# Channel attention into a gated feed-forward: the second chunk of v transposed on TensorE, and the last row group finished in two column halves

## The chip, the core and the metric

The kernel runs on one core of a Trainium2 chip. The metric is the device time of one execution in microseconds. A time is the median of several executions; the profile is of one execution.

## What is computed

Two stages follow each other. The first is channel attention over B = 4 batches of N = 6016 rows and C = 256 channels; the second is a feed-forward layer with a sigmoid gate over all 24064 rows, with 1536 hidden columns.

```
qn = q / (norm(q, axis=rows) + 1e-6)
kn = k / (norm(k, axis=rows) + 1e-6)
s  = kn.T @ qn / tau                       # 256 x 256 per batch, tau = 1
a  = softmax(s, last axis)
x  = v @ a                                 # 6016 x 256 per batch, rows of all batches joined
out = (sigmoid(x @ w_gate) * (x @ w_val)) @ w_out
```

Inputs and output are float32 in DRAM. The kernel computes its products in bfloat16 with float32 sums.

## The kernel before, in words

**Staging.** The product `v @ a` is never made by itself: for each batch the 256x256 matrix a is multiplied into the two weight matrices (`gh`: G = a w_gate and H = a w_val, in three column groups of 512, twelve pieces in all). What remains per batch is `sigmoid(v G) * (v H)` and the product with w_out. A batch has 47 row tiles of 128 rows, taken in NCH = 12 chunks: eleven of four tiles (512 rows) and a last one of three tiles (384 rows).

**A chunk.** `glu` (L404) does one of FC = 12 steps of a chunk, one for each 128 hidden columns: two products into a gate buffer and two into a val buffer of PSUM, each 512 columns wide, a sigmoid on ScalarE (L423) and a multiplication on VectorE (L424) that writes the hidden values hT. There are two gate buffers (pool psg) and two val buffers (psv), so a step can begin only when the step two before it has been read out of them. The moving operand of these products is v transposed, vT. `out_mms` (L430) does the product with w_out for the chunk before: per row tile twelve products of 256 columns, added up in one PSUM buffer (L440); `flush` (L446) copies the finished tile to SBUF on VectorE (L450) and, after the last tile of a chunk, stores the whole chunk from the SP queue (L452).

**Where vT comes from.** `load_v` (L103) loads a chunk of v through the GpSimd queue and casts it to bfloat16 on the way. `transpose_v` (L384) makes vT of it. It has two ways: a DMA transpose issued on SP (L391), or, when it is given a PSUM tile, eight TensorE products with the identity (L394) whose result is copied out in halves, one by VectorE (L398), one by ScalarE (L399; in the only call of this kind, for chunk 0 of batch 0, that copy is issued at L505).

**The order of work.** The schedule is written out by hand; every engine carries out its list in the order of the program. The start (L461 to L514) takes in q and k of batch 0, forms the scores and the softmax and the first five pieces of `gh`; the other seven follow the first seven glu steps of chunk 0 (L576, L577). In the loads' list on GpSimd come all q and k of batch 0, v of chunk 0, then the weights (L137 to L145): gate and val of column groups 0 and 1, v of chunk 1, gate and val of group 2, and w_out. `side_work` (L517) lists what is done beside the glu steps, by slot (chunk x 12 + step): the loads of v two chunks ahead, the transpose of v one chunk ahead (L529: at step 2 of each chunk, and for the first chunk of batch 0 at step 0), and all of the next batch's scores and norms. SP's list holds just the transposes and the stores, in turn.

**The end.** After the last chunk's glu steps nothing is left but its own out product: L585 to L587 go through its three row tiles, twelve products each, copy each tile, and store the three tiles together (384 KB).

Of the kernel before, what the change touches and what calls it, by code (L numbers as in the profile page):

```python
# [9 lines left out]
FP32 = mybir.dt.float32  # L10
BF16 = mybir.dt.bfloat16
# [6 lines left out]
def kernel(  # L18
# [20 lines left out]
    nc = tc.nc  # L39
    P = nc.NUM_PARTITIONS  # L40
# [4 lines left out]
    B, N, C = q.shape  # L45
# [3 lines left out]
    CB = C // P  # L49
    FC = DFF // P  # L50
    FG = 512
    NFG = DFF // FG
    TPC = 4
    CH = TPC * P
    NCH = (NT + TPC - 1) // TPC
    groups = [(t, min(TPC, NT - t)) for t in range(0, NT, TPC)]
# [4 lines left out]
    def rows(x, b):  # L61
        return x[b].rearrange("(p t) c -> p t c", p=P)

    out_rows = out.rearrange("(b p t) c -> b p t c", b=B, p=P)

    def pool(name, bufs, **kw):
        return ctx.enter_context(tc.tile_pool(name=name, bufs=bufs, **kw))
# [10 lines left out]
    opool = pool("opool", 2)  # L78
    psg = pool("psg", 2, space=PSUM)
    psv = pool("psv", 2, space=PSUM)  # L80
    pso = pool("pso", 2, space=PSUM)
    pss = pool("pss", 1, space=PSUM)
    psm = pool("psm", 1, space=PSUM)
# [19 lines left out]
    def load_v(b, ci):  # L103
        t0, nt = groups[ci]
        v_sb = vpool.tile([P, TPC, C], BF16, tag="v", name="v_sb")
        nc.gpsimd.dma_start(out=v_sb[:, :nt, :], in_=rows(v, b)[:, t0 : t0 + nt, :])  # L106
        vs[b, ci] = v_sb


    t0, nt = groups0[0]  # L110
# [24 lines left out]
    w_sb = [[consts.tile([P, CB, FG], BF16, name=f"w_{n}{fg}") for fg in range(NFG)] for n in ("gate", "val")]  # L135
    w_out_sb = consts.tile([P, FC, C], BF16)
    for fg in range(NFG):  # L137
        if fg == NFG - 1:
            load_v(0, 1)
        for w, src in enumerate((moe_w_gate, moe_w_val)):  # L140
            nc.gpsimd.dma_start(  # L141
                out=w_sb[w][fg],
                in_=src.rearrange("(t p) f -> p t f", p=P)[:, :, ds(fg * FG, FG)],
            )
    nc.gpsimd.dma_start(out=w_out_sb, in_=moe_w_out.rearrange("(t p) c -> p t c", p=P))  # L145


# [254 lines left out]
    hts = {}  # L402
# [25 lines left out]
    ffn = {}  # L428

    def out_mms(b, ci, n0, n1):  # L430

        t0, nt = groups[ci]
        hT = hts[b, ci]
        for n in range(n0, min(n1, nt * FC)):
            s, f = divmod(n, FC)
            if n == 0:
                ffn[b, ci] = opool.tile([P, TPC, C], FP32, tag="osb", name="out_sb")
            if f == 0:
                ffn["ps"] = pso.tile([P, C], FP32, tag="o", name="ps_o")
            mm(ffn["ps"], hT[:, f, ds(s * P, P)], w_out_sb[:, f, :], f == 0, f == FC - 1)  # L440
            if f == FC - 1:
                pending.append((ffn[b, ci], s, ffn["ps"], b, ci))
# [3 lines left out]
    def flush():  # L446
        while pending:
            out_sb, s, ps, b, ci = pending.pop(0)
            t0, nt = groups[ci]
            nc.vector.tensor_copy(out=out_sb[:, s, :], in_=ps)  # L450
            if s == nt - 1:
                nc.sync.dma_start(out=out_rows[b][:, t0 : t0 + nt, :], in_=out_sb[:, :nt, :])  # L452


    def busy(n):

        ps = psg.tile([P, CH], FP32, tag="g", name="ps_busy")
        for _ in range(n):
            mm(ps, ones_bf, ones_wide, True, True)
# [57 lines left out]
    def side_work(b):  # L517


        side = {}  # L520

        def at(slot, fn, *a):
            side.setdefault(divmod(slot, FC), []).append((fn, a))

        for ci in range(NCH):
            nb, nci = (b, ci + 1) if ci + 1 < NCH else (b + 1, 0)
            lb, lci = (b, ci + 2) if ci + 2 < NCH else (b + 1, ci + 2 - NCH)
            if nb < B:
                at(ci * FC + (0 if (b, ci) == (0, 0) else 2), transpose_v, nb, nci)  # L529
            if lb < B:  # L530
                at(ci * FC + 0, load_v, lb, lci)
        n = b + 1
        if n == B:
            return side
        first, last = (14 if b == 0 else 0), 8 * FC
        for g, (t0, nt) in enumerate(groups):
            s0 = first + g * (last - first) // NCH
            at(max(0, s0 - 20), load_qk, n, t0, nt)
            for u in range(nt):
                at(first + (t0 + u) * (last - first) // NT, score, n, t0, u)  # L540
            if g == 0:
                at(s0, acc_start, n)
            for i, (fn, w) in enumerate(((acc_square, 0), (acc_add, 0), (acc_square, 1), (acc_add, 1))):
                at(s0 + 1 + 2 * i, fn, n, g, w)
        for i in range(6):
            at(8 * FC + 2 + i, acc_fold, n, *divmod(i, 3))
        at(9 * FC + 9, norms_mm, n)
        for ci, s, *call in (
            (9, 0, wide_sqrt, n),
            (9, 2, wide_inv, n, 0),  # L550
            (9, 3, wide_inv, n, 1),
            (10, 0, wide_scale, n),
            (10, 0, exps, n, 0),
            (10, 0, exps, n, 1),
        ):
            side.setdefault((ci, FC + s), []).append((call[0], call[1:]))
        at(11 * FC + 0, sums_both, n)
        at(11 * FC + 0, gh_tiles, n)
        for i in range(len(gh_order)):
            at(11 * FC + min(i + 1, FC - 1), gh, n, i, *((pss, "s"), (psm, "m"))[i % 2])  # L560
        return side


    prev = None
    for b in range(B):
        side = side_work(b)
        for ci in range(NCH):
            block = b + 1 < B and ci in (9, 10)
            for f in range(FC):
                glu(b, ci, f)  # L570
                flush()
                if prev is not None and not block:
                    out_mms(*prev, f * TPC, (f + 1) * TPC)
                for fn, a in side.get((ci, f), ()):
                    fn(*a)
                if (b, ci) == (0, 0) and f < len(gh_order) - 5:  # L576
                    gh(0, 5 + f, pso, "o")  # L577
            if prev is not None and block:
                for s in range(TPC):
                    for fn, a in side.get((ci, FC + s), ()):  # L580
                        fn(*a)
                    out_mms(*prev, s * FC, (s + 1) * FC)
                    flush()
            prev = (b, ci)
    for s in range(groups[NCH - 1][1]):  # L585
        out_mms(*prev, s * FC, (s + 1) * FC)
        flush()  # L587


# [33 lines left out]
```

## Time and profile before

| what | us |
|---|---|
| median of 3 executions | 833.98 |
| the three executions | 835.4, 832.1, 833.98 |
| the profiled execution, its own time | 835.4 |
| span of the profiled execution, first to last instruction | 833.3 |
| busy: TensorE products | 816.1 |
| busy: VectorE | 588.5 |
| busy: ScalarE | 391.2 |
| DMA transposes on SP: 47; issue to landing, min / median / max | 3.3 / 3.7 / 16.8 |
| stores of out on SP: 48; issue to landing, min / median / max | 2.3 / 2.9 / 7.9 |

All times inside the profile are counted from the start of the span. The names in it are PE for TensorE's products, PEld for its weight loads, DVE for VectorE, ACT for ScalarE, POOL for GpSimd, SPq for SP's queue of DMA issues. A row such as `PE L88 MATMUL ps_gate<-vT,gh_G` means: a product at line 88 (the helper that issues every product) that writes ps_gate and reads vT and gh_G. Products overlap one another, so the time from one start to the next is shorter than the duration of one. In the DMA rows q0 is the queue of the loads that GpSimd issues, q1 that of SP.

### The profile page before, as it was taken

The page shows a single profiled execution, that of the slowest core. Times are in us where ns is not written, and L with a number is a line of the kernel's source. Part 1 is how long each engine was busy: PE and PEld are TensorE (multiplying, and loading weights), DVE is VectorE, ACT ScalarE, POOL GpSimd, SP SyncE. Part 2 cuts the span into 40 slices and gives each one's busy share as a digit, 9 for nine tenths or more (in the row PEclk, how much of TensorE's full clock was granted, in tenths as well). Part 3 has the DMA queues.
Part 4 walks back from the last instruction along what each step waited for, and adds up shares of the span by engine and source line. Part 5 has one row for each costly group of instructions (what it writes and reads, how often), then busy time and mean ns, then how long its engine had stood idle before and what let it go on. Part 6 is the DMA issues. An engine that isn't in the chain of part 4 may idle for free.

```text
span 833.3 us, 13748 instructions
## 1 busy us (share of the span) xinstructions
PE 816.1 (98%) x5184; PEld 502.0 (60%) x5198; DVE 588.5 (71%) x1021; ACT 391.2 (47%) x643; POOL 83.4 (10%) x159
## 2 busy tenths in 40 slices
PE   7889899999999999999999999999999999999998
PEld 4546566666665666665566666666566566666666
DVE  6567777787667777778767777777766666666664
ACT  4654344446644444444654444444655444444442
POOL 5522100002101100000221010000000000000000
PEclk9999999999999999999999999999999999999999
DMA  9999832335947423322975353223322423322111
GB/s 210 206 179 202 139 64 51 80 70 103 178 84 133 95 52 89 61 52 57 181 140 104 85 116 64 51 48 89 64 51 65 79 52 85 67 49 73 42 35 71
DMA packets 79794, 77.43 MB, mean 93 GB/s; under 512 B 51824, under 2 KB 56688, under 8 KB 79728
## 3 DMA queue, kind: packets, MB, share of 16 engines
q0 software_dynamic: 23920, 38.81, 28.6%
q1 hardware_dynamic: 55664, 37.23, 17.9%
q8 instruction: 40, 0.66, 0.3%
q10 hardware_dynamic: 144, 0.52, 0.2%
q14 instruction: 26, 0.21, 0.1%
HBM read 78.64 MB, written 24.64 MB: 124 GB/s over the span
## 4 chain that ended last, share of the span: by engine, by line
PE 90%; DMA 8%; DVE 1%; POOL 0%; issue 0%; ACT 0%; POOLq 0%
PE ps_o L88 29%; PE ps_gate L88 28%; PE ps_val L88 28%; DMA vT<-v_sb 4%; PE ps_s L88 3%; DMA k_sb<-in_k_dram 3%; PE ps_gh L88 2%; DMA v_sb<-in_v_dram 1%; DVE hT L424 0%; DVE sq L177 0%; ACT g_sb L423 0%; PE ps_n L88 0%; POOL q_sb L97 0%; POOL w_val L141 0%; POOL w_gate L141 0%
## 5 line engine op out<-in xcount | busy, mean ns | idle before, releaser
L424 DVE TENSOR_TENSOR hT<-ps_val,g_sb 128x512 bf16<-128x512 f32 (+1 forms) x576 | 391.3, 680 | 210.2 <-ACT g_sb L423 206.2
L423 ACT ACTIVATE g_sb<-ps_gate 128x512 bf16<-128x512 f32 (+1 forms) x576 | 338.3, 588 | 391.2 <-PE ps_gate L88 384.3
L88 PE MATMUL ps_gate<-vT,gh_G 128*128 128x512 bf16 (+1 forms) x1152 | 337.6, 375 | 4.9 <-DMA vT<-v_sb 4.6
L88 PE MATMUL ps_val<-vT,gh_H 128*128 128x512 bf16 (+1 forms) x1152 | 337.5, 375 | 0.3
L88 PE MATMUL ps_o<-w_out_sb,hT 128*128 128x256 bf16 x2256 | 326.1, 273 | 0.0
L88 PEld LDWEIGHTS <-hT 128*128 128x128 bf16 x2256 | 220.7, 98 | 124.8
L88 PEld LDWEIGHTS <-gh_H 128*128 128x128 bf16 x1152 | 112.7, 98 | 131.6 <-issue 0.8
L88 PEld LDWEIGHTS <-gh_G 128*128 128x128 bf16 x1152 | 112.3, 98 | 43.1 <-DMA vT<-v_sb 5.4
L106 POOL DMA_DIRECT2D v_sb<-in_v_dram x48 | 25.6, 532 | 621.5 <-DMA vT<-v_sb 527.3
L450 DVE COPY out_sb<-ps_o 128x256 f32<-128x256 f32 x188 | 77.8, 414 | 13.5 <-PE ps_o L88 13.5
L88 PE MATMUL ps_s<-k_sb,q_sb 128*128 128x256 bf16 x376 | 66.0, 272 | 5.4 <-DMA k_sb<-in_k_dram 4.3
L88 PEld LDWEIGHTS <-q_sb 128*128 128x128 bf16 x376 | 36.6, 98 | 14.1 <-issue 6.6
L216 DVE TENSOR_TENSOR acc<-acc,sq 128x1024 bf16<-128x1024 bf16 (+1 forms) x66 | 44.2, 669 | 0.0
L177 DVE TENSOR_TENSOR sq<-q_sb 128x1024 bf16<-128x1024 bf16 (+2 forms) x44 | 29.4, 667 | 2.6 <-DMA q_sb<-in_q_dram 2.6
L97 POOL DMA_DIRECT2D k_sb<-in_k_dram x48 | 26.2, 546 | 20.1 <-DMA k_sb<-in_k_dram 8.2
L97 POOL DMA_DIRECT2D q_sb<-in_q_dram x48 | 26.7, 555 | 14.3 <-DMA q_sb<-in_q_dram 7.0
L177 DVE TENSOR_TENSOR sq<-k_sb 128x1024 bf16<-128x1024 bf16 (+2 forms) x34 | 22.4, 658 | 0.9 <-ACT sq L175 0.9
L377 ACT ACTIVATE gh_G<-ps_gh,rrow 128x512 bf16<-128x512 f32 x21 | 14.4, 687 | 12.7 <-PE ps_gh L88 8.8
L88 PE MATMUL ps_busy<-ones_wide,ones_bf 128*128 128x512 bf16 x57 | 16.6, 418 | 1.7 <-DVE shift L127 1.6
L175 ACT ACTIVATE sq<-k_sb 128x1024 bf16<-128x1024 bf16 (+1 forms) x11 | 11.2, 1018 | 14.8 <-DMA k_sb<-in_k_dram 13.4
L379 DVE TENSOR_SCALAR gh_H<-ps_gh,rrow 128x512 bf16<-128x512 f32 x22 | 16.4, 743 | 1.6 <-PE ps_gh L88 1.6
L473 DVE TENSOR_TENSOR acc<-acc,sq 128x1024 bf16<-128x1024 bf16 x16 | 11.1, 692 | 5.5 <-ACT sq L175 5.2
(64 smaller groups left out, 122.2 us busy)
## 6 DMA issues: line engine op xcount, KB each, us to landing
out_dram<-out_sb SPq DMA_DIRECT2D x44, 512.0 KB, 2.9
v_sb<-in_v_dram POOLq DMA_DIRECT2D x44, 256.0 KB, 3.8
q_sb<-in_q_dram POOLq DMA_DIRECT2D x43, 256.0 KB, 7.3
k_sb<-in_k_dram POOLq DMA_DIRECT2D x43, 256.0 KB, 8.1
out_dram<-out_sb SPq DMA_DIRECT2D x4, 384.0 KB, 2.7
w_gate<-in_moe_w_gate_dram POOLq DMA_DIRECT2D x3, 256.0 KB, 6.8
w_val<-in_moe_w_val_dram POOLq DMA_DIRECT2D x3, 256.0 KB, 7.4
w_out_sb<-in_moe_w_out_dram POOLq DMA_DIRECT2D x1, 768.0 KB, 17.3
```

Source lines behind the costliest of these rows:

```text
L88: nc.tensor.matmul(out, lhsT=lhsT, rhs=rhs, start=start, stop=stop, **kw)
L97: nc.gpsimd.dma_start(out=tl[:, :nt, :], in_=rows(src, b)[:, t0 : t0 + nt, :])
L106: nc.gpsimd.dma_start(out=v_sb[:, :nt, :], in_=rows(v, b)[:, t0 : t0 + nt, :])
L175: nc.scalar.activation(out=sq[:, :nt, :], in_=src[:, :nt, :], func=ACT.Square)
L177: engine.tensor_tensor(out=sq[:, :nt, :], in0=src[:, :nt, :], in1=src[:, :nt, :], op=ALU.mult)
L216: nc.vector.tensor_tensor(out=acc[:, :nt, :], in0=acc[:, :nt, :], in1=st[b]["sq", w][:, :nt, :], op=ALU.add)
L377: nc.scalar.activation(out=dst, in_=ps, func=ACT.Copy, scale=r)
L379: nc.vector.tensor_scalar(out=dst, in0=ps, scalar1=r, scalar2=None, op0=ALU.mult)
L423: nc.scalar.activation(out=g_sb[:, :n], in_=ps_gate[:, :n], func=ACT.Sigmoid)
L424: nc.vector.tensor_tensor(out=hts[b, ci][:, f, :n], in0=ps_val[:, :n], in1=g_sb[:, :n], op=ALU.mult)
L450: nc.vector.tensor_copy(out=out_sb[:, s, :], in_=ps)
L473: nc.vector.tensor_tensor(out=acc[w], in0=acc[w], in1=sq[w], op=ALU.add)
```

## The change

Two edits are made together.

1. The load of v for chunk 1 of batch 0 moves in GpSimd's list from ahead of the weights of column group 2 to behind them. Its transpose is done by TensorE, after glu step 7 of chunk 0, into the PSUM tile of pool psm, and copied out by VectorE and ScalarE, in place of the DMA transpose that SP issued at step 0.
2. The third and last row tile of the whole kernel is done by a new function, `last_rows`. The first two tiles of the last chunk are stored by themselves. The products of the last tile are done in two halves of 128 output columns, each with its own PSUM buffer, copied by VectorE into a small tile of its own, and stored separately, the first from SP's queue, the second from ScalarE's.

```diff
     for fg in range(NFG):
-        if fg == NFG - 1:
-            load_v(0, 1)
         for w, src in enumerate((moe_w_gate, moe_w_val)):
             nc.gpsimd.dma_start(
                 out=w_sb[w][fg],
                 in_=src.rearrange("(t p) f -> p t f", p=P)[:, :, ds(fg * FG, FG)],
             )
+    load_v(0, 1)
     nc.gpsimd.dma_start(out=w_out_sb, in_=moe_w_out.rearrange("(t p) c -> p t c", p=P))
...
+    def last_rows(b, ci):
+
+        t0, nt = groups[ci]
+        s, half = nt - 1, C // 2
+        hT = hts[b, ci]
+        nc.sync.dma_start(out=out_rows[b][:, t0 : t0 + s, :], in_=ffn[b, ci][:, :s, :])
+        for n, queue in enumerate((nc.sync, nc.scalar)):
+            ps = pso.tile([P, half], FP32, tag="o", name="ps_end")
+            for f in range(FC):
+                mm(ps, hT[:, f, ds(s * P, P)], w_out_sb[:, f, ds(n * half, half)], f == 0, f == FC - 1)
+            end = opool.tile([P, half], FP32, tag=f"end{n}", name="end", bufs=1)
+            nc.vector.tensor_copy(out=end, in_=ps)
+            queue.dma_start(out=out_rows[b][:, t0 + s, ds(n * half, half)], in_=end)
...
-            if nb < B:
-                at(ci * FC + (0 if (b, ci) == (0, 0) else 2), transpose_v, nb, nci)
+            if (nb, nci) == (0, 1):
+                at(7, lambda: transpose_v(0, 1, psm.tile([P, TPC * CB, P], BF16, tag="m", name="ps_tp")))
+            elif nb < B:
+                at(ci * FC + 2, transpose_v, nb, nci)
...
-    for s in range(groups[NCH - 1][1]):
+    for s in range(groups[NCH - 1][1] - 1):
         out_mms(*prev, s * FC, (s + 1) * FC)
         flush()
+    last_rows(*prev)
```

## The prediction, made before the changed kernel had run

> **What bounds the kernel now.** I read the page first, then the waits, then the timelines of the two places that the change touches. The first and fourth parts of the page:
>
> ```profile
> PE 816.1 (98%) x5184; PEld 502.0 (60%) x5198; DVE 588.5 (71%) x1021; ACT 391.2 (47%) x643; POOL 83.4 (10%) x159
> PE 90%; DMA 8%; DVE 1%; POOL 0%; issue 0%; ACT 0%; POOLq 0%
> ```
>
> TensorE is busy for 98% of the span and carries 90% of the chain that ended last. It does as much work after the change, so only its gaps, and what follows its last product, can be won. The page's PEclk row is 9 in all slices and the mean clock is 0.999: no term for the clock. The waits of TensorE between 30 and 120 us (who waited for what, us in total, times, longest):
>
> ```profile
> PE ps_gate L88 <- DMA vT<-v_sb: 4.6, 2, 2.4
> PE ps_s L88 <- DMA k_sb<-in_k_dram: 0.7, 1, 0.7
> ```
>
> Two waits for a transposed v. The timeline around the first, at the start of chunk 1 of batch 0 (start, us, instruction, idle before it):
>
> ```profile
> 51.97 0.59 PE L88 MATMUL ps_gate<-vT,gh_G 128*128 128x512 bf16 x2
> 52.84 0.53 POOL L106 DMA_DIRECT2D v_sb<-in_v_dram  x1 [7.99 <-DMA w_out_sb<-in_moe_w_out_dram]
> 54.03 1.23 SPq L391 DMA_TRANSPOSE vT<-v_sb  x1
> 55.27 0.60 PE L88 MATMUL ps_gate<-vT,gh_G 128*128 128x512 bf16 x2 [2.27 <-DMA vT<-v_sb]
> ```
>
> Between 49.37 and 51.97 a glu step takes 0.867 us, so chunk 1 could begin at 51.97+0.87 = 52.84. It begins at 55.27: **stall 1 costs 2.43 us**. The transpose it waits for was issued at 41.28 and landed 13.9 us later. **Stall 2** is at chunk 3:
>
> ```profile
> 88.88 0.60 PE L88 MATMUL ps_o<-w_out_sb,hT 128*128 128x256 bf16 x4
> 91.86 0.61 PE L88 MATMUL ps_gate<-vT,gh_G 128*128 128x512 bf16 x2 [2.38 <-DMA vT<-v_sb]
> ```
>
> The four ps_o take 4 x 0.109 = 0.44 us, so chunk 3 could begin at 89.32; it loses **2.54 us**. Its transpose was issued at 74.97, behind a store that waited for TensorE's own results until 74.50, and took 16.8 us. The median of all 47 is 3.7 us: these early ones share the DMA engines with the backlog of loads. The tail:
>
> ```profile
> 827.85 0.43 DVE L450 COPY out_sb<-ps_o 128x256 f32<-128x256 f32 x1 [0.89 <-PE ps_o L88]
> 829.16 0.42 DVE L450 COPY out_sb<-ps_o 128x256 f32<-128x256 f32 x1 [0.88 <-PE ps_o L88]
> 829.61 0.33 SPq L452 DMA_DIRECT2D out_dram<-out_sb  x1
> out_dram<-out_sb SPq DMA_DIRECT2D x1, 512.0 KB, 2.6
> out_dram<-out_sb SPq DMA_DIRECT2D x1, 384.0 KB, 2.3
> ```
>
> The last product reaches VectorE at 829.16, the last store is issued at 829.61 and lands 2.3 us on, at 831.9. Then 1.4 us of closing work up to 833.3, which the change leaves.
>
> **Part 1, the transpose.** *Removed:* one DMA transpose on SP; SP then has nothing ahead of chunk 2's transpose but that one's own wait for v, which ends at 54.03. *Moved:* v of chunk 1 behind two weight loads on GpSimd's queue. Two issues of 0.70 us go ahead of its own, but the transfers decide: it takes the place of the second weight load, which had landed when GpSimd's wait for w_val ended at 44.32. The new transpose needs it at 49.37: 5 us of cover, and a later landing would cost one for one beyond it. The weight load moves forward; it was not waited for. GpSimd's later loads each wait for the eighth load before them, and the places keep their bytes.
>
> *Added on TensorE:* eight products after glu step 7. The row for the same eight at L394 is 0.61 us for all and 0.219 for one, so they start (0.61-0.219)/7 = 0.056 us apart: 8 x 0.056 = **0.45 us**, on the path.
>
> *Added behind them:* the copies. VectorE's 128x512 copy took 0.42 us (L398), ScalarE's 0.56 (L505); in the changed instruction list ScalarE's half waits for VectorE's. VectorE begins hT of step 7 at 49.88 and is free at 50.5, so it copies until 50.9 and ScalarE until 51.5. Queued behind it is step 8's sigmoid: it begins at 51.4 instead of the 50.45 that its product allows, and ends at 52.0. TensorE wants that gate buffer (there are two) for step 10 at 49.37 + 0.45 + 2 x 0.867 = 51.55, and waits 0.5 us; hT of step 8 ends at 52.72, so step 10's val products wait about 0.27 more. Bounds for this knock-on: 0 (if the slack holds, as now) and 0.98 (both copies in full); I take 0.77. Chunk 1 begins at 52.84+0.45+0.77 = 54.06, **1.2 us earlier**. w_out, needed 0.9 us later, had landed by 52.84.
>
> *What is late next:* stall 2. TensorE would ask for chunk 3 at 89.32-1.21 = 88.11. How far does its transpose move? The loads' queue, with and without the removed transpose beside it (44 to 56 us, then 71 to 77; packets, MB, share):
>
> ```profile
> q0 software_dynamic: 1786, 2.02, 102.1%
> q1 hardware_dynamic: 1056, 0.26, 19.8%
> ...
> q0 software_dynamic: 690, 1.26, 112.5%
> ```
>
> Alone the loads move 0.21 MB/us; beside the transpose they moved 2.02 MB in 12 us where 2.52 would go. The removal frees 0.5/0.21 = 2.4 us of backlog; by the rate of 41 to 44 us (0.20) it is 1.9. If the DMA engines are the limit up to 91.8, which their share of over 9 tenths until about 86 speaks for, chunk 3's transpose lands 1.9 to 2.4 us earlier. If its length is fixed, it lands just 1.2 earlier, as its issue does. If traffic no longer holds it up, stall 2 goes and the gain there is 1.21+2.54 = 3.75. Nearest to the rows is the first: **2.1 us** at chunk 3, with 0 and 3.75 as ends (0: the landing does not move). After it transposes take 9.6 us and less against 17 us of chunk, so the gain stays up to the tail.
>
> **Part 2, the tail.** The last 12 products of 0.109 (1.31 us) become 24 of half the width. Nearest row: the 128x128 pairs above, 0.056 apart, so 1.34 in all; upper bound 24 x 0.109 = 2.62. I take 0.056, since it is a stream of pairs of the same size. TensorE: Matmul & The Clock Gate, section Back-to-back issue gap, in the Trainium skill, speaks against this: it gives about 81 ns for each pair at 128 columns in a real kernel, which would make 1.94 us and take 0.6 us from the gain; no stream of such products into one accumulator is in this trace.
>
> The first half reaches VectorE at 827.85+0.67 = 828.52, when the copy of the row before is done (828.28); the second at 829.19. No 128x128 copy out of PSUM is shown; between 0.21 (L256) and 0.41 (L450) I take 0.28, the 128x128 f32 operation at L309. The last store is then issued at 829.19+0.28+0.03 = 829.50 on ScalarE's queue, idle since its last sigmoid (about 825), 0.11 us earlier than now. Landing: 512 KB took 2.6 and 384 KB 2.3 us, a line that gives 64 KB 1.55 us; ends 2.3 (no shorter) and 4.8 (the one transfer that this queue shows, 512 KB at the start of the kernel). I take 1.55: landed at 831.05, **0.85 us earlier**; ends +1.1 (the cheapest copy and a landing of 1.4) and -2.4. On SP the store of the other two rows goes out at 828.31 and the first half at 828.83; both land before. DMA: Bandwidth & Descriptors, section Issuing engines are not separate DMA queues, in the Trainium skill, says a second issuing engine saves only the issue time; by that the second queue itself is worth at most the 0.33 us row, and the rest of this term is the smaller size.
>
> **Sum.** 2.1 + 0.85 = 2.95 us. The profiled execution took 835.4 us (span 833.3 and 2.1 around it), so 832.45 by its own time. It was the longest of the three runs; against the median of 833.98 the same sum gives **831.0**. If its extra 1.4 us lay in these very stalls, the gain against the median is only 1.5.
>
> **Rivals.**
> - *Stall 2 goes.* For: 2.3 us more backlog freed beside the shift; for chunk 4 a transpose took 9.6 us. Against: while issued earlier, it meets nearly the same queue. 3.75 + 0.85 = 4.6 us: 829.4. Chance 0.2.
> - *Stall 2 takes the gain back*, the wait only changing its place: chunk 3's transpose still lands at 91.8, because the freed DMA time goes to loads that were waiting to be issued (the 7.99 us of GpSimd speak for it; the engines' full share against). Gain 0 + 0.6 to 0.85: 833.3. Chance 0.15.
> - *Slower: chunk 2's transpose becomes the late one.* It was issued at 54.03, took 15.9 us and was needed at 72.35; now it is needed at 71.14. While it ran, the DMA engines moved only 109 to 121 GB/s between 59 and 65 us, so it may stretch. It stalls TensorE beyond 17.1 us, which none reached. Landing at 78 (24 us) puts chunk 2 off by 5.65 us against now; stall 2 (2.54) is then covered and the tail gives 0.85: 2.3 us slower, 836.2. It passes today's time from a landing at 75.7, and 0.5% from 79.9. Chance 0.08, half of it beyond 0.5%.
> - The forecast: 0.57, from 829.9 to 832.5.
>
> **Numbers.** A measurement of this kernel tells 0.5% (4.2 us) from no change. Faster by more: 0.2 and 0.03 from the edge of the forecast; slower: 0.04; within: 0.73. The range takes in both ends at chunk 3 and, with the forecast there, the slow end of the last store (834.3), and reaches 0.6 below 828.9 for the scatter of the medians: 828.3 to 834.4.
>
> **What the changed profile would show.** TensorE's wait for vT at chunk 1 gone, eight ps_tp after step 7 within 0.45 us, a gap of some 0.8 us about step 10; chunk 1 at 54.1; chunk 3 at 89.8, with a wait of about 1.6 us for its transpose; the last store issued 0.1 us earlier against the last product's place and landing in 1.6. Wrong if v of chunk 1 lands after 49.4, if the half products stand 0.08 us or more apart, or if a wait for vT of 3 us or more stands at chunk 2 or 3.

## The result, and the profile after

| kernel | median us | executions | lowest to highest |
|---|---|---|---|
| before | 834.25 | 6 | 832.1 to 836.04 |
| changed | 830.59 | 6 | 830.48 to 831.27 |

The ratio is 0.9959, with a 95% interval of 0.9942 to 0.9975: 3.7 us less, within the 0.5% (4.2 us) that the prediction counts as no change, though the interval leaves out 1. The predicted time was 831.0. The scatter changed too: 3.9 us between the executions of before, 0.8 us between those after.

The profiled execution of the changed kernel took 831.27 us, with a span of 829.2, against 835.4 and 833.3: 4.1 us less. The first and fourth parts of its page, as they were shown of before:

```profile
PE 816.6 (98%) x5204; PEld 502.9 (61%) x5218; DVE 588.7 (71%) x1023; ACT 391.6 (47%) x644; POOL 83.0 (10%) x159
PE 94%; DMA 4%; DVE 1%; issue 0%; POOL 0%; ACT 0%; POOLq 0%; ACTq 0%
```

TensorE has 0.5 us more work, the eight transposes, and yet the span is shorter. DMA's share of the chain that ended last fell from 8% to 4%: the gaps went. The waits of TensorE between 30 and 130 us (for what, us in total, times, longest):

```profile
PE ps_s L88 <- DMA k_sb<-in_k_dram: 0.7, 1, 0.7
PE ps_gh L88 <- DMA w_val<-in_moe_w_val_dram: 0.4, 1, 0.4
PE ps_gate L88 <- ACT g_sb L422: 0.4, 1, 0.4
```

Both waits for vT are gone, the one at chunk 3 included. Two small ones are new: one for a weight tile, one for a sigmoid. The timeline of the changed kernel around glu steps 7 to 10 (start, us, instruction, idle before it):

```profile
49.88 0.61 PE L393 MATMUL ps_tp<-ident_bf,v_sb 128*128 128x128 bf16 x8
50.33 0.59 PE L88 MATMUL ps_gate<-vT,gh_G 128*128 128x512 bf16 x2
51.44 0.58 ACT L398 COPY vT<-ps_tp 128x512 bf16<-128x512 bf16 x1 [1.19 <-DVE vT L397]
51.92 1.09 ACT L422 ACTIVATE g_sb<-ps_gate 128x512 bf16<-128x512 f32 x2
52.58 0.59 PE L88 MATMUL ps_gate<-vT,gh_G 128*128 128x512 bf16 x2 [0.36 <-ACT g_sb L422]
53.31 0.59 PE L88 MATMUL ps_val<-vT,gh_H 128*128 128x512 bf16 x2
54.60 0.59 PE L88 MATMUL ps_gate<-vT,gh_G 128*128 128x512 bf16 x2
```

The eight transposes hold TensorE for 0.45 us. ScalarE's copy waits 1.19 us for VectorE's, the sigmoid of step 8 stands behind it until 51.92, and step 10 begins at 52.58 instead of 52.06, its val products another 0.30 us late. Chunk 1 begins at 54.60. Chunk 3 begins at 88.64, with no wait, against 91.86 before:

```profile
88.64 0.59 PE L88 MATMUL ps_gate<-vT,gh_G 128*128 128x512 bf16 x2
```

The end, with the last 24 products, the copies and the last issue in the timeline:

```profile
824.48 1.51 PE L88 MATMUL ps_end<-w_out_sb,hT 128*128 128x128 bf16 x24
824.68 0.42 DVE L449 COPY out_sb<-ps_o 128x256 f32<-128x256 f32 x1 [0.89 <-PE ps_o L88]
825.36 0.29 DVE L464 COPY end<-ps_end 128x128 f32<-128x128 f32 x1 [0.25 <-PE ps_end L88]
826.03 0.29 DVE L464 COPY end<-ps_end 128x128 f32<-128x128 f32 x1 [0.39 <-PE ps_end L88]
826.35 0.35 ACTq L465 DMA_DIRECT2D out_dram<-end  x1
```

and the DMA issues of the same stretch (size, us to landing):

```profile
out_dram<-end SPq DMA_DIRECT2D x1, 64.0 KB, 1.9
out_dram<-end ACTq DMA_DIRECT2D x1, 64.0 KB, 1.6
```

From the copy of the last but one tile (824.68) to the end of the span it is 4.52 us, against 833.3-827.85 = 5.45 before. So the two profiles put 0.93 us at the tail and 827.85-824.68 = 3.17 us ahead of it, all of which is there at chunk 3 (91.86-88.64 = 3.22).

### The profile page after: what moved, and what is told of

It reads as the page before. It is cut to its first block, busy times and chain, and to the rows that moved or that the text cites. A ratio compares the mean times of both kernels' runs of the same rounds, so it can differ in the third digit from the quotient of the medians.

```text
span 829.2 us, 13794 instructions
## 1 busy us (share of the span) xinstructions
PE 816.6 (98%) x5204; PEld 502.9 (61%) x5218; DVE 588.7 (71%) x1023; ACT 391.6 (47%) x644; POOL 83.0 (10%) x159
## 4 chain that ended last, share of the span: by engine, by line
PE 94%; DMA 4%; DVE 1%; issue 0%; POOL 0%; ACT 0%; POOLq 0%; ACTq 0%
PE ps_o L88 30%; PE ps_gate L88 29%; PE ps_val L88 29%; PE ps_s L88 4%; DMA k_sb<-in_k_dram 3%; PE ps_gh L88 2%; DMA w_val<-in_moe_w_val_dram 1%; DVE hT L423 0%; ACT g_sb L422 0%; DVE sq L176 0%; PE ps_end L88 0%; POOL q_sb L97 0%; PE ps_n L88 0%; POOL w_gate L139 0%; POOL k_sb L97 0%
```

## The experiments

Each kernel was timed beside the kernel before on its own chip, in three groups. The ratios are to that kernel; its median differed between the groups (836.75, 835.97, 837.06), while the changed kernel, timed again, came out the same. So the size of the gain depends on the executions of before that it is set against: 3.7 us in the result above, 6.4 us (837.06 against 830.63) in the last group.

| kernel | median us | ratio, 95% interval |
|---|---|---|
| tail alone | 834.77 | 0.9984, 0.9966 to 1.0003 |
| start alone | 830.97 | 0.9941, 0.992 to 0.9963 |
| old load order | 830.84 | 0.9938, 0.9918 to 0.9958 |
| spare transpose | 830.45 | 0.9937, 0.9917 to 0.9958 |
| spare transpose, old order | 834.06 | 0.9973, 0.9952 to 0.9994 |
| before, chunk 3's transpose early | 832.65 | 0.9967, 0.995 to 0.9983 |
| later copy | 830.0 | 0.9934, 0.9911 to 0.9958 |
| spare transpose later, old order | 830.66 | 0.993, 0.9904 to 0.9957 |
| last row whole | 830.95 | 0.9933, 0.9911 to 0.9956 |
| one queue | 830.86 | 0.9937, 0.9909 to 0.9964 |
| changed kernel again | 830.63 | 0.9929, 0.9903 to 0.9955 |

The question was why stall 2 went, of which the prediction had left 1.6 us. My theory was the DMA time that the removed transpose had taken; the rivals were chance, the order of the loads, and the shifted issues.

**The tail alone.** The kernel before with

```diff
-    for s in range(groups[NCH - 1][1]):
+    for s in range(groups[NCH - 1][1] - 1):
         out_mms(*prev, s * FC, (s + 1) * FC)
         flush()
+    last_rows(*prev)
```

> The kernel before with the tail edit alone (last row tile in column halves, two queues). My theory takes the change apart into a start worth 3.2 us and a tail worth 0.93 us in the two profiles. It expects 0.9 us less than before (about 833.3), and from the copy of the last but one row tile to the end of the span 4.5 us as in the changed kernel, against 5.45 before, with stall 1 and stall 2 still there. The rival, that the two edits are not independent (a tail that is only shorter because the stores of a less crowded end land sooner), expects less than 0.4 us.

Measured: 834.77 beside 836.75; the interval takes in 1. Both stalls are there (idle 2.25 us at 55.12, 1.77 at 91.10). In its profile it is 831.5-827.09 = 4.41 us from the last but one copy to the end, 1.0 less than before. The mechanism is as expected; its size does not stand out of the scatter that the stalls make.

**The start alone.** The changed kernel with the same lines taken back:

```diff
-    for s in range(groups[NCH - 1][1] - 1):
+    for s in range(groups[NCH - 1][1]):
         out_mms(*prev, s * FC, (s + 1) * FC)
         flush()
-    last_rows(*prev)
```

> The changed kernel with the tail of before: the transpose on TensorE and the moved load alone. Theory: both waits for vT are gone, so about 831.5 by the median (0.9 above the changed kernel), and a spread of the runs below 1 us, as in the changed kernel. Rival: the second stall went by chance in the one profile; then some runs lie 2 us or more above the others, and a wait for vT at chunk 3 can show here.

Measured: 830.97, all six executions within 0.62 us, no wait for vT. Nearly the whole gain and the whole calm are the start's. Chunk 1 begins at 53.92, 1.20 us ahead of its place in the tail-alone kernel (55.12). Chunk 3 begins at 87.96; the wait for w_val that the first profile of the changed kernel showed is absent here. The tail is worth 0.36 us by the medians (830.97 against 830.6, in different groups), not 0.9: the same tail as before's took 4.99 us to the end in this profile, not 5.45. The other profiles with the old tail have 5.44 to 5.45 (three), those with the new one 4.41 to 4.89 (eight), so the tail is worth 0.1 us to 1.0 and its size stays open. SP waited 1.5 us for the last store instead of 1.9, though its landing shows 2.3 in both; why is open.

**The old load order.** The changed kernel with

```diff
     for fg in range(NFG):
+        if fg == NFG - 1:
+            load_v(0, 1)
...
-    load_v(0, 1)
     nc.gpsimd.dma_start(out=w_out_sb, ...)
```

> The changed kernel with v of chunk 1 loaded where it was before, ahead of the weights of column group 2, and still transposed by TensorE. In the changed kernel TensorE waited 0.37 us for w_val of group 1 (started 40.75 against 40.23), which landed 8.1 us after its issue instead of 7.4. Theory A: this is a price of the move, and goes: the wait for w_val 0, the piece of gh after glu step 0 at 40.2, and 0.4 to 0.5 us less than the changed kernel (830.1). Theory B: it is scatter of the loads; then it can stay, and the times are the same within 0.2 us. If the move of the load was what removed stall 2, that stall is back and the kernel 2 us slower.

Measured: 830.84, no wait for vT. Theory A falls: the wait for w_val is absent here, but also with the moved load in the start-alone and spare-transpose kernels and in the second profile of the changed kernel. It is scatter of one execution. The load order alone is worth nothing that shows.

**A spare transpose.** The changed kernel with the removed DMA transpose back on SP, its result read by nobody:

```diff
+    def spare_transpose():
+        spare = consts.tile([P, TPC * CB, P], BF16, name="spare")
+        nc.sync.dma_start_transpose(out=spare, in_=vs[0, 1].rearrange("p t c -> p (t c)"))
...
+                at(0, spare_transpose)
                 at(7, lambda: transpose_v(0, 1, ...))
```

> The changed kernel with one DMA transpose of v of chunk 1 put back on SP at the place of before, into a tile that nobody reads; TensorE still makes the vT that is used. Nothing waits for it, so only its traffic is back. Theory (the DMA time of one transpose is what makes the later ones land late): w_out and v of chunk 2 land 2 to 4 us later than in the changed kernel, chunk 3's transpose takes over 14 us again instead of 10.9, stall 2 is back in part, 1 to 3 us slower than the changed kernel (831.6 to 833.6). Rival (stall 2 went because the issues moved, or by the load order): no wait for vT, same time as the changed kernel within 0.3 us.

Measured: 830.45, no wait for vT. **My theory fell**, at least in this form: the traffic of one transpose does not bring stall 2 back. The DMA queues of this kernel from 44 to 56 us (packets, MB, share):

```profile
q0 software_dynamic: 1887, 2.25, 107.2%
q1 hardware_dynamic: 792, 0.20, 12.2%
```

Without it the loads (q0) moved 2.40 MB here, before the change 2.02. From 44 to 70 us the sums are 4.68 MB with the spare transpose, 4.97 without, and 3.94 before: the traffic as such costs 0.3 MB or 1.4 us of loads, the transpose of before cost 1.0 MB.

What else differs is when its packets run. In this kernel the first is in the slice from 47 to 48 us, when w_out has just landed (GpSimd's wait for it ends at 48.07). In the kernel before they begin in the slice from 45 us, in the middle of w_out's 1 KB rows. (The sizes in these rows are those after the cast to bfloat16, so a row of 1 KB counts 0.5 KB.) Its slices 46 to 47 and 51 to 52 us:

```profile
q0 software_dynamic: 220, 0.14, 91.4%
q1 hardware_dynamic: 218, 0.06, 41.4%
...
q0 software_dynamic: 95, 0.17, 97.4%
q1 hardware_dynamic: 91, 0.02, 18.4%
```

Packet for packet, the two queues take turns. Against rows of 4 KB (the second slice, 0.17 MB in 95 packets) a transpose gets 0.02 MB/us, and the loads fall from 0.21 MB/us to 0.17; against rows of 1 KB it gets 0.06, and they fall from 0.20 to 0.14.

**The spare transpose at its old time.** The same, with the old load order, so that SP issues it at 41.3:

```diff
     for fg in range(NFG):
+        if fg == NFG - 1:
+            load_v(0, 1)
...
-    load_v(0, 1)
```

> The changed kernel with v of chunk 1 loaded in its old place and a DMA transpose of it on SP at the old time, into a tile that nobody reads: the traffic of the kernel before, without its wait. The spare transpose behind the moved load (issued at 43.8) did nothing, and its first packet ran at 47.9, after w_out had landed; in the kernel before the packets begin at 45, beside w_out, whose landing goes from 47.9 to 52.5. Theory now: what makes the later transposes late is a transpose that runs beside w_out's 1 KB rows, packet for packet. It expects w_out at 52 again, the loads' queue at about 2.0 MB in 44 to 56 us, chunk 3's transpose late with a wait of TensorE of 1 to 4 us (it asks 1.2 us earlier than before), and 832 to 834 us. Rival (TensorE's own stall of 2.4 us at chunk 1, which held up the loads that wait for its results, made the rest late): no wait at chunk 3 and 830.6.

Measured: 834.06, and the executions scatter from 831.1 to 836.7, as before the change. TensorE does not wait for the spare result, but stall 2 is back, longer in this profile (of an execution of 835.54 us) than it was:

```profile
PE ps_gate L88 <- DMA vT<-v_sb: 3.3, 1, 3.3
```

GpSimd's wait for w_out ends at 53.85 (before 52.84, changed 48.21) after 9.01 us. Then, in the slice from 59 to 60 us, with chunk 2's transpose begun:

```profile
q1 hardware_dynamic: 208, 0.05, 101.6%
q0 software_dynamic: 20, 0.04, 30.0%
```

The loads get 20 packets in a microsecond where they had 95 to 115. From 56 to 70 us they move 1.22 MB; before it was 1.92, in the changed kernel 2.57. That is the backlog in which chunk 3's transpose is late: it was issued at 73.70, no later than in the start-alone kernel (73.63), and took 17.7 us instead of 10.7. How it ends shows in two other slices. In the changed kernel the loads run dry between 81 and 82 us (33 packets); the transpose gets 503 packets there and lands at 85.2, 3.4 us before it is needed. In the kernel before, the loads still move 81 packets between 86 and 87 us, and the transpose lands at 91.8.

The trace shows one thing more. Behind this wait of 3.27 us TensorE runs at half speed for some 3 us; a pair of products takes 1.06 us instead of 0.59:

```profile
94.27 1.06 PE L88 MATMUL ps_val<-vT,gh_H 128*128 128x512 bf16 x2
```

The granted clock is 0.50 between 93 and 95 us and 1.00 again from 96. The products from 91.47 to 95.98 take 4.51 us, the same row of products behind them 2.82, so the clock costs 1.7 us on top of the wait. In the two profiles of the kernel before, after waits of 2.3 to 2.7 us, the clock stayed at 1.00.

**The spare transpose a little later, at the old order.** It transposes the last weight tile, which has landed by 43.8:

```diff
-        nc.sync.dma_start_transpose(out=spare, in_=vs[0, 1].rearrange("p t c -> p (t c)"))
+        nc.sync.dma_start_transpose(out=spare, in_=w_sb[1][NFG - 1].rearrange("p t c -> p (t c)"))
```

> As the run with the spare transpose at the old load order (TensorE makes the vT that is used; the spare result is read by nobody), but the spare transposes the last loaded weight tile (gate/val group 2, same size) instead of v of chunk 1, so that SP issues it when that has landed, near 43.8 and not at 41.3. The load order is the old one. Theory (what hurts is a transpose whose packets run beside w_out's 1 KB rows): the first packet is at about 47.6, w_out lands by 48.5, no wait at chunk 3, and 830.4 to 831.0, as with the spare transpose behind the moved load. Rival (the old load order together with any transpose of this time does it): w_out at 52, a wait at chunk 3, 833 to 835.

Measured: 830.66, no wait for vT, GpSimd's wait for w_out over at 48.16. From 44 to 56 us:

```profile
q0 software_dynamic: 1895, 2.25, 107.3%
q1 hardware_dynamic: 794, 0.20, 12.3%
```

It is the spare-transpose kernel again, at the other load order. So not the order and not the amount, but the 2.5 us by which the transpose begins earlier, beside w_out, makes stall 2. That w_out's short rows are the reason, and that the slow stretch after 58 us comes from GpSimd's longer pause in issuing loads (nothing new between 44.9 and 52.8 us before), fits all runs, but neither was tried by itself: both stay arguments.

**Chunk 3's transpose early, in the kernel before.**

```diff
-                at(ci * FC + (0 if (b, ci) == (0, 0) else 2), transpose_v, nb, nci)
+                at((0 if (b, ci) == (0, 0) else 22 if (b, ci) == (0, 2) else ci * FC + 2), transpose_v, nb, nci)
```

> The kernel before with one edit: chunk 3's transpose stands in SP's list ahead of the store of chunk 0 (slot 22 in place of 26), so that it is issued when its v has landed (about 63) and not behind a store that waits for TensorE's results (74.5). Theory: stall 2 is a matter of this late issue into a crowded queue; chunk 3's transpose lands by 85, the second wait is gone, stall 1 stays, and 2 to 2.5 us come off the kernel before of the same call. Rival: the queue is what is late, and a transpose issued earlier only slows the loads and with them chunk 2's transpose; then less than 1 us.

Measured: 832.65, 3.3 us under before's 835.97, somewhat more than expected, and ten of twelve executions within 0.74 us. The one wait for vT that is left is stall 1:

```profile
PE ps_gate L88 <- DMA vT<-v_sb: 2.4, 1, 2.4
```

So stall 2 had a second condition: the issue behind a store that waits for TensorE's results.

**A later copy.** The changed kernel with ScalarE's half of the copy one step later:

```diff
-                at(7, lambda: transpose_v(0, 1, psm.tile(...)))
+                at(7, lambda: transpose_v(0, 1, psm.tile(...), lambda *a: late.append(a)))
+                at(8, lambda: nc.scalar.copy(*late.pop()))
```

> The changed kernel with ScalarE's half of the vT copy one glu step later in its list, behind step 8's sigmoid in place of ahead of it. In the changed kernel that half waited 1.19 us for VectorE's half, step 8's sigmoid behind it began at 51.9 and TensorE waited 0.36 and then some 0.3 us at step 10. Theory: both waits go, chunk 1 begins 0.8 us earlier, 829.8 us. Rival: the wait moves to step 11 or to the start of chunk 1, whose products need vT and step 10's buffers; then less than 0.2 us.

Measured: 830.0, 0.6 us under the changed kernel's 830.59 and 830.63 (in other groups): the lowest median of this study, by less than the scatter of its executions (829.37 to 831.68). Its timeline shows the mechanism:

```profile
50.44 0.60 ACT L422 ACTIVATE g_sb<-ps_gate 128x512 bf16<-128x512 f32 x1 [0.71 <-PE ps_gate L88]
50.93 0.58 ACT L545 COPY vT<-ps_tp 128x512 bf16<-128x512 bf16 x1
51.53 0.59 PE L88 MATMUL ps_gate<-vT,gh_G 128*128 128x512 bf16 x2
53.26 0.59 PE L88 MATMUL ps_gate<-vT,gh_G 128*128 128x512 bf16 x2
```

Step 8's sigmoid goes first, step 10 begins at 51.53, where the prediction had put it without a wait (51.55), and chunk 1 at 53.26, 0.66 us ahead of the start-alone kernel, although its transposes began 0.15 us later (49.36 against 49.21): from the transposes to chunk 1 it is 3.90 us instead of 4.71.

**The kernel before, profiled again.**

> The kernel before, for another profile of it. If the two waits for vT are how this kernel runs, stall 1 and stall 2 are there again at 55 and 92 us, within 1 us of the first profile, and the loads' queue slows to 0.1 MB a us between 58 and 65. If stall 2 was one execution's accident, it is absent here.

Measured: 835.55, with both waits in place:

```profile
55.16 0.61 PE L88 MATMUL ps_gate<-vT,gh_G 128*128 128x512 bf16 x2 [2.34 <-DMA vT<-v_sb]
92.07 0.61 PE L88 MATMUL ps_gate<-vT,gh_G 128*128 128x512 bf16 x2 [2.70 <-DMA vT<-v_sb]
```

Stall 2 was no accident. The dip of the loads is there as well, shallower (138 to 178 GB/s in the slices from 58 to 64 us).

Neither profile of before is of a long execution. Of its 56 executions in the three groups, the twelve above 838 us show a mean granted clock of 0.995 to 0.997, the five below 833 us 0.999 or 1.0. So its scatter is in part the clock; that the clock falls behind a longer stall 2 there, as in the spare transpose at its old time, is likely but not shown, since no trace of a long execution was kept.

**The last row whole, and one queue.** In the changed kernel's `last_rows`, twelve products of 256 columns, one copy, one store of 128 KB on SP:

```diff
-        for n, queue in enumerate((nc.sync, nc.scalar)):
...
+        ps = pso.tile([P, C], FP32, tag="o", name="ps_end")
+        for f in range(FC):
+            mm(ps, hT[:, f, ds(s * P, P)], w_out_sb[:, f, :], f == 0, f == FC - 1)
+        end = opool.tile([P, C], FP32, tag="end", name="end", bufs=1)
+        nc.vector.tensor_copy(out=end, in_=ps)
+        nc.sync.dma_start(out=out_rows[b][:, t0 + s, :], in_=end)
```

> The changed kernel with the last row tile not halved: twelve products of 256 columns, one copy of 128x256 (0.42 us), one store of 128 KB on SP behind the store of the other two tiles. It tells the smaller last store from the halves. By the rows: the copy ends 0.13 us later than the second half's, the store of 128 KB lands in about 1.75 us against 1.6 on ScalarE's queue: 0.25 to 0.3 us slower than the changed kernel, so two thirds of the tail's 0.93 us come from the split store alone. Rival: the halves and the second queue are what counts, then 0.6 us or more slower.

and, with the halves kept,

```diff
-        for n, queue in enumerate((nc.sync, nc.scalar)):
+        for n, queue in enumerate((nc.sync, nc.sync)):
```

> The changed kernel with both half stores on SP. In its profile SP issued the first half's store at 825.67 for 0.64 us, until 826.31, and the second half was copied at 826.32; so the second store would be issued at the same time from SP. Theory: the second queue is worth nothing, the same time within 0.15 us. Rival: the second store queues behind the first on SP, whose landing took 1.9 us, and the end is 0.3 to 0.6 us later.

Measured: 830.95 and 830.86, against 830.63 in the same group: 0.32 and 0.23 us slower. From the last but one copy to the end it is 4.77 and 4.73 us, against 4.55. For the whole row the size was as expected. How the tail's gain divides stays open: by the medians the whole row ends where the start-alone kernel does (830.97, in another group), which would leave everything to the halves; by the profiles the store split off is worth 0.2 us (4.99 in the start-alone kernel) or 0.7 (5.45 in the kernel before), the halves 0.2. The second queue is worth 0.2 us by the medians and the profiles, less than the 0.33 us that the prediction allowed it at most: with one queue, SP spends 1.23 us on issuing the two stores,

```profile
825.36 1.23 SPq L465 DMA_DIRECT2D out_dram<-end  x2
825.72 0.29 DVE L464 COPY end<-ps_end 128x128 f32<-128x128 f32 x1 [0.38 <-PE ps_end L88]
```

and is through at 826.59, where ScalarE's issue, 0.35 us from the copy's end at 826.01, would be through by 826.4.

**The changed kernel again.**

> The changed kernel again, on the chip of the three others, for their comparison: 830.6, spread under 1.5 us, no wait of TensorE for vT in batch 0, and whether the wait for w_val of group 1 (0.37 us in its first profile, absent in three other runs with the same loads) shows.

Measured: 830.63, from 830.21 to 830.85, no wait for vT and none for w_val.

## Why the prediction was right, point by point

- *Part 1, on TensorE.* Eight products 0.056 us apart, 0.45 us: as measured. The knock-on was put at 0.77 us; it is 0.52+0.30 = 0.82, and the later copy takes it away (3.90 us instead of 4.71 from the transposes to chunk 1), which shows the cause. Chunk 1 "1.2 us earlier": 1.20 between the start-alone and the tail-alone kernel; only 0.67 in the first profile of the changed kernel, where the piece of gh that waited for w_val began 0.52 us late (40.75 against 40.23).
- *The moved load.* v of chunk 1 had landed when GpSimd's wait for it ended at 44.42, its products began at 49.88: 5.5 us of cover, where 5 were predicted.
- *Stall 2.* **This is the term that was mis-sized.** The prediction said "Nearest to the rows is the first: 2.1 us at chunk 3", with 1.6 us of the wait left. It is 3.2 us with none left. In the start-alone kernel, without the wait for w_val, chunk 3 begins at 87.96, 3.90 us earlier than before; 0.16 of that stands already at the first step of chunk 0 (39.07 against 39.23), and what is left is the upper end that had been kept (3.75). I had counted the removed transpose as an amount of traffic in the stretch from 44 to 56 us, 1.9 to 2.4 us. As an amount it is worth 1.4 us and removes no wait; what counted was that it ran beside w_out. And the larger part of the loss came after that stretch: against the changed kernel the loads are 0.38 MB behind from 44 to 56 us, and another 0.65 MB from 56 to 70. The row that could have told it was there: GpSimd's 7.99 us of waiting for w_out, which I put down as a point for the opposite rival.
- *The tail.* The pairs of 128 columns stand (1.51-0.219)/23 = 0.056 us apart, as the transposes' row said, and not 0.081 as TensorE: Matmul & The Clock Gate, section Back-to-back issue gap, in the Trainium skill, gives for a real kernel: here the page and the measurement differ, and the measurement decides. The copy took 0.29 (0.28 predicted), the last store landed in 1.6 (1.55). Predicted 0.85 us; 0.93 between the first two profiles, 0.36 by the medians of the start-alone and the changed kernel: the parts were right, the size of the whole is not settled.
- *The sum.* 2.95 predicted; 4.1 between the profiled executions, 3.7 between the medians. That the median came out 0.4 us from the forecast is partly luck. The case that happened at chunk 3 is the rival "stall 2 goes", which had a chance of 0.2 and the time 829.4; a tail that gave less by the medians made up for part of it. And the forecast was taken off a median of before that moves from 833.98 to 837.06 between groups.
- *The clock.* The prediction had "no term for the clock", from one profile in which it stayed at full speed. In the long executions of before it did not, as their mean granted clock shows, and part of what the changed kernel gains against them lies there.
- *The rivals on the other side.* Chunk 2's transpose was issued at 49.17, landed at 65.3 and was never late. In the kernel with the spare transpose at its old time chunk 3's was late again.

## What to carry to other kernels

Here a transpose of small packets cost the other transfers by when it ran, and not by its bytes: look at the loads in flight beside it, at their row size, and at who waits for the load that it delays, before counting bytes. A wait that appears far behind its cause, and a scatter between executions, can have one source; putting the suspected traffic back without its wait is a cheap way to find it. An operation that two engines share should be queued behind the work that others wait for, not ahead of it.

## What the runs showed of the hardware that was not expected

- Two DMA queues with packets ready took turns packet by packet: 220 to 218 beside 1 KB rows, 95 to 91 beside 4 KB rows. A DMA transpose of 1056 packets therefore took some 11 us of packets beside waiting loads (97 a us), where the median of all transposes is 3.7 us from issue to landing.
- Between the issue of such a transpose and its first packet it was about 4 us in this crowd (41.3 to 45, 43.8 to 47.9).
- A shift of 2.5 us in one transpose that nobody waits for moved the median by 3.4 us (834.06 against 830.66) and the scatter of the executions from 1.5 to 5.6 us.
- After an idle of 3.27 us TensorE's granted clock fell to 0.50 for some 3 us; after 2.3 and 2.7 us it did not.
